# Q's first half copied in four banks by two engines, group 0's sums and first normalize moved ahead of V's projections, and group 1's values moved behind the first FFN matmuls, in the opening of a Linformer attention + squared-ReLU FFN kernel

## The chip, the cores and the metric

One core of one Trainium2 chip. The metric is device microseconds for one execution of the whole kernel. All runs told here are of the fast kind (no run was more than 1.5% above the fastest of its kernel), and the times of kernels are compared over the runs of the same rounds on the same chip.

## The reference, cut to what matters

```python
k_proj = einsum('ks,bhsd->bhkd', E, k)          # E, F: 64 x 1024; q, k, v: 8 x 8 x 1024 x 64
v_proj = einsum('ks,bhsd->bhkd', F, v)
attn   = softmax(q @ k_proj^T / sqrt(64))       # 1024 x 64 for each batch and head
x      = (attn @ v_proj) as 8192 rows of 512
out    = square(relu(x @ w_in)) @ w_out         # 512 -> 2048 -> 512
```

The attention is small. The two matrix products behind it are the work. Of the eight batches, only the first must do its attention before the FFN can begin; the others do it in the shadow of the FFN of the batch before. The first batch is cut into two halves of its columns, and only the first half of its attention stands ahead of the first FFN matmul. The change is all in that opening.

## The kernel before

The opening, in program order (in the timelines of the two kernels TensorE, VectorE and ScalarE each show their instructions in this order; where TensorE waits, what follows waits too: in the changed kernel V's projection, whose load had landed at 16.86 us (17.10 less the lag of 0.24 us, both below), starts at 18.21 us, behind sums that started at 17.98):

```python
for s in (slice(0, 4), slice(4, 8)):
    load_heads(K_first, k, s)                     # one load queue, in this order
...
load_q_half(0, slice(0, H))
for s in (slice(0, 4), slice(4, 6), slice(6, 8)):
    load_heads(V_first, v, s)
... # then w_in in pieces, the second half of Q, w_out

def half_transpose_q(self, c, g, psum):           # four heads into one PSUM bank, one copy
    ps = psum("ps_q", (P, 4, 2, P), BF16)
    for h in range(4):
        for n in range(2):
            nc.tensor.transpose(ps[:, h, n], self.Q[:, 4 * g + h, ...], ident[:])
    nc.vector.tensor_copy(qt[:, 4 * g:4 * g + 4, 2 * c:2 * c + 2], ps[:])

def first_stages(self):
    filler(2); self.project_k(0)                  # filler(n): n matmuls whose result nobody reads
    filler(1); self.transpose_k(0)
    self.project_k(1)
    filler(2); self.transpose_k(1)
    filler(1)
    for g in range(2):
        self.half_transpose_q(0, g, ffn_psum)
    for g in range(2):                            # g: four heads
        self.half_scores(0, g)
        self.half_exponentials(g)                 # ScalarE
    heads = [slice(0, 4), slice(4, 6), slice(6, 8)]
    self.project_v(heads[0])                      # waits for V's load
    self.copy_v(heads[0])
    self.half_sums(0, apart=True)                 # waits for exponential 0
    self.half_sums(1)
    self.half_reciprocals(0)                      # ScalarE: Ln, then Exp(-x)
    self.half_reciprocals(1)
    self.half_values(0)
    for s in heads[1:]:
        self.project_v(s)
        self.copy_v(s)
    self.half_values(1)
    for g in range(2):
        for e in range(2):
            self.half_normalize(0, g, e)          # VectorE; writes block 2g+e of xT
# then the FFN: the first 16 matmuls into ps_h are four output blocks, taken
# column block by column block of xT: four matmuls need only normalize (0,0),
# the next four (0,1), then (1,0), then (1,1).
```

The instructions that carry the story are: the Q transposes (`ps_q`), the scores and exponential 0, the projection of V (`ps_v`), the sums (`ps_r`), the values, and the first `ps_h`.

The softmax here doesn't subtract the row's maximum and nothing guards it: scores larger than these inputs give would overflow.

## Time and profile before

| | before |
|---|---|
| median of 3 runs | 484.47 us (483.62 to 485.47) |
| span of the profiled run | 482.4 us |
| TensorE busy | 470.3 us (97%) |
| TensorE's waits, summed | 8.3 us, all up to 21.05 us |
| first `ps_h` / 17th `ps_h` | 21.05 us / 24.70 us |

From the page of the kernel before, its first and fourth part:

```profile
## 1 busy us (share of the span) xinstructions
PE 470.3 (97%) x3630; PEld 292.6 (61%) x3630; DVE 314.1 (65%) x382; ACT 261.5 (54%) x413; POOL 34.7 (7%) x48
...
## 4 chain that ended last, share of the span: by engine, by line
PE 92%; DVE 3%; DMA 3%; ACT 1%; POOL 1%; issue 0%; POOLq 0%
```

TensorE (PE) is the limit, so a gain must be TensorE time that comes earlier. The waits of TensorE in the kernel before (columns: what waited and for what, us in total, times, longest):

```profile
PE ps_E L144 <- DVE e_bf L140: 5.0, 1, 5.0
PE ps_E L144 <- ACT e_bf L140: 1.8, 1, 1.8
PE ps_kT L271 <- DVE kp L265: 0.6, 2, 0.3
PE ps_att L307 <- DVE qT L299: 0.5, 2, 0.3
PE ps_h L459 <- DVE xT L351: 0.2, 1, 0.2
PE ps_att L320 <- DVE vp L288: 0.2, 1, 0.2
```

These six are all that the view lists, and the last of them ends at 21.05 us. TensorE's timeline of the opening (columns: start, duration, line, what it wrote and read, shapes, count; in brackets idle time before it and what ended it):

```profile
9.11 1.92 PE L262 MATMUL ps_k<-K_sb,ET 128*64 128x256 bf16 x8
...
12.00 1.06 PE L262 MATMUL ps_k<-K_sb,ET 128*64 128x256 bf16 x8
...
14.29 1.07 PE L296 MATMUL ps_q<-ident,Q_sb 128*128 128x128 bf16 x16
15.69 0.41 PE L307 MATMUL ps_att<-qT,kT 64*64 64x256 bf16 x8 [0.33 <-DVE qT L299]
...
16.82 1.06 PE L284 MATMUL ps_v<-V_sb,FT 128*64 128x256 bf16 x16
17.82 0.30 PE L320 MATMUL ps_r<-expT,ones 64*32 64x256 bf16 x8
...
18.75 1.32 PE L284 MATMUL ps_v<-V_sb,FT 128*64 128x128 bf16 x32
...
21.05 6.40 PE L459 MATMUL ps_h<-xT,w_in 128*128 128x512 bf16 x28 [0.19 <-DVE xT L351]
...
53.03 0.40 PE L180 MATMUL ps_kv<-K_sb,ET 128*64 128x512 bf16 x1
53.32 0.38 PE L181 MATMUL ps_kv<-V_sb,FT 128*64 128x512 bf16 x1
```

The first `ps_v` line starts at 16.82 us because V's load lands then. (The last two lines, `ps_kv`, belong to the projection of K and V of batch 1.) When loads land can be read from the engine that issues them (POOL), which waits for an older load to end before it issues another (1.83 us for V's first part before it issues at 17.06). Its timeline of the same run:

```profile
14.53 0.70 POOL L124 DMA_DIRECT2D w_in<-in_moe_w_in_dram  x1 [1.92 <-DMA Q_sb<-in_q_dram]
17.06 0.77 POOL L97 DMA_DIRECT2D Q_sb<-in_q_dram  x1 [1.83 <-DMA V_sb<-in_v_dram]
...
19.67 0.71 POOL L124 DMA_DIRECT2D w_in<-in_moe_w_in_dram  x1 [0.56 <-DMA V_sb<-in_v_dram]
...
22.33 0.71 POOL L124 DMA_DIRECT2D w_in<-in_moe_w_in_dram  x1 [0.52 <-DMA w_in<-in_moe_w_in_dram]
```

The engine notices V at 17.06, TensorE at 16.82: a lag of 0.24 us. So Q landed at about 14.29, V's first part at 16.82, V's last part at 19.43 (V comes in three loads), and w_in's third load (the one that the ninth `ps_h` needs) at 22.09.

### The profile page before, as it was taken

To read this page: it belongs to the slowest core of one execution; us is meant where nothing else is said; L and a number is where in the kernel's file an instruction comes from. 1 tells how busy PE (TensorE), PEld (TensorE's weight loads), DVE (VectorE), ACT (ScalarE), POOL (GpSimd) and SP (SyncE) were. 2 spreads that over 40 slices of the span, in tenths; PEclk is the share of its full clock that TensorE was granted. 3 is DMA by queue.
4 is the path that set the end of the run, shared out by engine and by line. 5 is a ranking of instruction groups with operands and counts; after the bars stand their busy time and mean duration, and the time that the engine had idled before them with its cause. 6 is when DMAs were issued, how large, how long until landed. Compare 5 with 4: busy or idle time off the path is not lost.

```text
span 482.4 us, 8423 instructions
## 1 busy us (share of the span) xinstructions
PE 470.3 (97%) x3630; PEld 292.6 (61%) x3630; DVE 314.1 (65%) x382; ACT 261.5 (54%) x413; POOL 34.7 (7%) x48
## 2 busy tenths in 40 slices
PE   4899999999999999999999999999999999999997
PEld 2544676475574746657475665747557474666656
DVE  1478955554958559493776848667494855948383
ACT  2387544758427564466635667176662756545351
POOL 6540020020020001000010000100000000000000
PEclk9999999999999999999999999999999999999999
DMA  9999989579989086941859147690702102020202
GB/s 155 203 204 207 168 181 200 137 120 229 180 128 229 12 175 88 180 94 50 153 86 227 22 115 131 91 200 1 165 11 75 25 1 88 1 88 0 88 1 87
DMA packets 72789, 55.46 MB, mean 115 GB/s; under 512 B 33968, under 2 KB 64944, under 8 KB 72752
## 3 DMA queue, kind: packets, MB, share of 16 engines
q0 software_dynamic: 30624, 29.36, 39.4%
q1 hardware_dynamic: 42128, 25.56, 21.1%
q8 instruction: 28, 0.46, 0.4%
q14 instruction: 9, 0.07, 0.0%
HBM read 59.24 MB, written 16.78 MB: 158 GB/s over the span
## 4 chain that ended last, share of the span: by engine, by line
PE 92%; DVE 3%; DMA 3%; ACT 1%; POOL 1%; issue 0%; POOLq 0%
PE ps_h L459 44%; PE ps_y L479 23%; PE ps_z L479 11%; PE ps_x L479 6%; DMA V_sb<-in_v_dram 3%; PE ps_kv L180 2%; PE ps_att L221 2%; PE ps_att L206 2%; DVE hsq L521 1%; DVE s L473 1%; PE ps_v L284 0%; DVE xT L246 0%; DVE xT L351 0%; PE ps_kv L181 0%; ACT h_relu L513 0%; POOL K_sb L93 0%
## 5 line engine op out<-in xcount | busy, mean ns | idle before, releaser
L459 PE MATMUL ps_h<-xT,w_in 128*128 128x512 bf16 x1024 | 224.8, 379 | 0.2 <-DVE xT L351 0.2
L521 DVE TENSOR_TENSOR hsq<-h_relu 128x1024 bf16<-128x1024 f32 x123 | 149.9, 1222 | 75.0 <-ACT h_relu L513 74.2
L513 ACT ACTIVATE h_relu<-ps_h 128x512 f32<-128x512 f32 x255 | 149.4, 597 | 63.4 <-PE ps_h L459 63.0
L459 PEld LDWEIGHTS <-w_in 128*128 128x128 bf16 x1024 | 99.7, 98 | 117.7 <-issue 1.9
L479 PEld LDWEIGHTS <-s 128*128 128x128 bf16 x1024 | 98.5, 98 | 19.8 <-issue 8.7
L479 PEld LDWEIGHTS <-hsq 128*128 128x128 bf16 x768 | 73.8, 98 | 17.3 <-issue 3.8
L479 PE MATMUL ps_y<-T,s 128*128 128x256 bf16 x512 | 62.4, 273 | 0.0
L246 DVE TENSOR_TENSOR xT<-ps_att,rs 128x1024 bf16<-128x1024 f32 x28 | 33.4, 1215 | 17.6 <-ACT rs L236 17.0
L473 DVE TENSOR_TENSOR s<-hsq 128x1024 bf16<-128x1024 bf16 x64 | 43.5, 683 | 0.0
L591 ACT COPY o_sb<-ps_y 128x512 f32<-128x512 f32 x15 | 8.8, 586 | 53.8 <-PE ps_y L479 53.7
L213 ACT ACTIVATE expT<-ps_att 128x1024 bf16<-128x1024 f32 x28 | 27.2, 1025 | 14.0 <-PE ps_att L206 14.0
L479 PE MATMUL ps_x<-w_out,hsq 128*128 128x256 bf16 x256 | 33.2, 273 | 0.0
L479 PE MATMUL ps_y<-w_out,hsq 128*128 128x256 bf16 x256 | 33.2, 273 | 0.0
L595 DVE TENSOR_TENSOR o_sb<-ps_z,p_b 128x512 f32<-128x512 f32 x16 | 11.0, 688 | 33.8 <-issue 19.9
L479 PE MATMUL ps_y<-T,hsq 128*128 128x256 bf16 x256 | 30.9, 272 | 0.0
L479 PE MATMUL ps_z<-T,s 128*128 128x256 bf16 x256 | 30.6, 273 | 0.0
L479 PE MATMUL ps_z<-w_out,s 128*128 128x256 bf16 x256 | 30.6, 273 | 0.0
L591 ACT COPY p_b<-ps_y 128x512 f32<-128x512 f32 (+1 forms) x17 | 9.4, 556 | 25.9 <-PE ps_y L479 25.8
L81 POOL DMA_DIRECT2D Q_sb<-in_q_dram x7 | 6.1, 876 | 227.7 <-DMA qT<-Q_sb 227.2
L473 DVE TENSOR_TENSOR s<-s,hsq 128x1024 bf16<-128x1024 bf16 x32 | 21.8, 684 | 0.3
L473 DVE TENSOR_TENSOR s<-hsq,s 128x1024 bf16<-128x1024 bf16 x32 | 21.7, 682 | 0.0
L591 ACT COPY p_a<-ps_y 128x512 f32<-128x512 f32 (+1 forms) x17 | 9.4, 561 | 21.8 <-PE ps_y L479 21.6
(75 smaller groups left out, 233.0 us busy)
## 6 DMA issues: line engine op xcount, KB each, us to landing
out_dram<-o_sb SPq DMA_DIRECT2D x30, 512.0 KB, 3.8
K_sb<-in_k_dram POOLq DMA_DIRECT2D x7, 1024.0 KB, 15.3
V_sb<-in_v_dram POOLq DMA_DIRECT2D x7, 1024.0 KB, 22.4
Q_sb<-in_q_dram POOLq DMA_DIRECT2D x7, 1024.0 KB, 9.4
w_out<-in_moe_w_out_dram POOLq DMA_DIRECT2D x4, 512.0 KB, 13.2
w_in<-in_moe_w_in_dram POOLq DMA_DIRECT2D x7, 256.0 KB, 10.0
K_sb<-in_k_dram POOLq DMA_DIRECT2D x2, 512.0 KB, 8.5
out_dram<-o_sb SPq DMA_DIRECT2D x3, 256.0 KB, 2.1
```

The lines of the kernel that those rows point to most:

```text
L180: nc.tensor.matmul(ps[0:KP, :], lhsT=ET[:, i, :], rhs=kv[:, :, i, :], start=f, stop=l)
L206: nc.tensor.matmul(ps[o, bank, :], lhsT=self.kT[r, 2 * pr + j, :], start=True, stop=True, rhs=self.qT[r, NT * (2 * pr + j):NT * (2 * pr + ...
L213: nc.scalar.activation(e[:], self.ps["s", pr][:], AF.Exp, scale=SCALE)
L221: nc.tensor.matmul(ps[32 * j:32 * j + 32, a, :], lhsT=weights(o, 4 * g + j), rhs=self.exp[2 * g + j // 2][o, bank, :], start=True, stop=Tr ...
L246: nc.vector.tensor_tensor(out=self.xT[:, 2 * g + e].rearrange("p a n t -> p a (n t)"), in0=self.ps["v", g, e][:], in1=self.rs[g][:], op=AL ...
L459: nc.tensor.matmul(ps[:], lhsT=w_in_blk(cb, fb), rhs=xT[:, cb, :, 2 * ch:2 * ch + 2], start=(cb == 0), stop=(cb == NCB - 1),)
L473: nc.vector.tensor_tensor(out=s[o][:, js], in0=x, in1=y, op=op)
L479: nc.tensor.matmul(ps[tb] if len(ps) == 2 else ps[0][:, tb], lhsT=lhs[:, j, tb * P:(tb + 1) * P], rhs=rhs[:, j], start=first and n == 0 an ...
L513: nc.scalar.activation(r[:, n], ps[:], AF.Relu)
L521: multiply = lambda: nc.vector.tensor_tensor(out=o, in0=r[:], in1=r[:], op=ALU.mult)
L591: nc.scalar.copy(to[:, t], ps)
L595: nc.vector.tensor_tensor(out=to[:, t], in0=ps, in1=more[:, t], op=ALU.add)
```

## The change

The intent: split the copies of Q over two engines and four banks, so that scores start sooner; let group 0's sums, which need only Q and K, run before V's projection; and let the first `ps_h` start behind normalize (0,0) and (0,1), with group 1's values and normalizes between the first `ps_h` matmuls. One filler ahead of the Q transposes is dropped as well.

```diff
-        def half_transpose_q(self, c, g, psum):
-            ps = psum("ps_q", (P, 4, 2, P), BF16)
-            for h in range(4):
+        def half_transpose_q(self, c, hs, psum, copy):
+            ps = psum("ps_q", (P, len(hs), 2, P), BF16)
+            for m, h in enumerate(hs):
                 for n in range(2):
                     nc.tensor.transpose(
-                        ps[:, h, n], self.Q[:, 4 * g + h, (2 * c + n) * P:(2 * c + n + 1) * P], ident[:])
+                        ps[:, m, n], self.Q[:, h, (2 * c + n) * P:(2 * c + n + 1) * P], ident[:])
             qt = self.qT[:].rearrange("p (h n) t -> p h n t", n=NT)
-            nc.vector.tensor_copy(qt[:, 4 * g:4 * g + 4, 2 * c:2 * c + 2], ps[:])
+            copy(qt[:, hs.start:hs.stop, 2 * c:2 * c + 2], ps[:])
@@ first_stages
             self.transpose_k(1)
-            filler(1)
-            for g in range(2):
-                self.half_transpose_q(0, g, ffn_psum)
+            for n in range(4):
+                self.half_transpose_q(
+                    0, range(2 * n, 2 * n + 2), ffn_psum, nc.scalar.copy if n == 1 else nc.vector.tensor_copy)
             for g in range(2):
                 self.half_scores(0, g)
                 self.half_exponentials(g)
             heads = [slice(0, 4), slice(4, 6), slice(6, 8)]
+            self.half_sums(0, apart=True)
             self.project_v(heads[0])
             self.copy_v(heads[0])
-            self.half_sums(0, apart=True)
             self.half_sums(1)
             self.half_reciprocals(0)
             self.half_reciprocals(1)
             self.half_values(0)
+            self.half_normalize(0, 0, 0)
             for s in heads[1:]:
                 self.project_v(s)
                 self.copy_v(s)
+            self.half_normalize(0, 0, 1)
+
+        def last_of_first(self):
             self.half_values(1)
-            for g in range(2):
-                for e in range(2):
-                    self.half_normalize(0, g, e)
+            for e in range(2):
+                self.half_normalize(0, 1, e)
@@ SECOND_HALF (what is called ahead of which step of the FFN)
-        7: "second_half 0 0", ...
+        1: "last_of_first", 7: "second_half 0 0", ...
```

(The second half's call of `half_transpose_q` is adapted and does what it did.)

## The prediction

> **What bounds the kernel.** TensorE: 470.3 us busy of a span of 482.4 (page), and 92% of the chain of waits that ended last. The view of TensorE's waits lists 8.4 us of idle time in the whole run, all before the first `ps_h` matmul at 21.05 us; from 21.05 to 37.40 TensorE is busy 16.22 of 16.35 us, from 60 to 440 us 379.89 of 380 (windows). So the change, which touches only the first 40 us, can gain no more than it brings forward the moment from which TensorE runs feed-forward matmuls without a gap.
>
> **What leads up to that moment (timeline).** Q transposes 14.29 (Q's load lands about then), two VectorE copies of 128x1024 14.95 to 16.24, scores 15.69 and 16.29, exponentials on ScalarE 16.15 to 18.09, V's projection 16.82 (waits for V's load), values of group 0 18.41, V's last heads 19.43 to 20.09, their copy until 20.40, values of group 1 until 20.87, first normalize 20.32, first `ps_h` 21.05.
>
> **What the change does, costed.**
> - Q copies: one filler less (no gain: Q lands when it ended). Four 128x512 copies, VectorE about 0.42 each, ScalarE 0.59 (the ET and FT copies of this shape). Heads 0-1 are ready about 15.2, heads 2-3 only at 15.6, ScalarE being the slower copier; the first exponential starts about 16.0 instead of 16.15.
> - Group 0's sums ahead of V: they wait for exponential 0 (about 17.05), and TensorE takes matmuls in order, so V's projection moves from 16.82 to about 17.25: 0.4 us lost for V, its copies and values. [...]
> - Normalize (0,0) moves ahead of the last V copies: about 19.35, 1 us earlier.
> - The first four `ps_h` matmuls (4 x 0.217) start right behind V's projection, which now ends about 20.5 instead of 20.05. Values of group 1 (about 0.4 us of issue) run behind them, their normalizes hidden under `ps_h`.
>
> Result: first `ps_h` about 20.5, one 0.4 us interruption, so the fifth output block (17th `ps_h`) starts about 24.35 instead of 24.70. Net gain about 0.3 us, 0.07%, all on the critical path. With half the loss to V it would be 0.5; if normalizes (1,0), (1,1) (0.65 us each) come late, 0.1.
>
> **Limit from below.** w_in's loads are nearly just in time: from when the issuing engine's waits for slots end, less the 0.24 us lag seen for V, I estimate landings at 20.1, 20.75, 22.1, 23.35, 24.6. A start earlier by over 0.5 us would wait for them.
>
> **Predicted: 484.1 us, 8 in 10 between 483.2 and 485.0**; the spread of before's runs (483.62 to 485.47) is larger than the effect. Faster by over 2%: 0.005; within 2%: 0.99; slower: 0.005.
>
> **What would show it.** Timeline: V's projection starts at 17.1 to 17.4, released by ScalarE (not by V's load); first exponential 15.9 to 16.1; first `ps_h` 20.3 to 20.8; values of group 1 between the fourth and fifth `ps_h`; the 17th `ps_h` at 24.2 to 24.5. From 40 us on both traces are the same but for the shift.
>
> **What would make it wrong.** V's or w_in's loads landing later than estimated (TensorE then waits for a DMA after 20 us); new PSUM waits (the fourth `ps_h` needs the bank of V's last copy); ScalarE's copy being quicker than 0.59; a later stage of the first batch absorbing the shift.

The sum came to a first `ps_h` at about 20.5 us and a 17th at about 24.35 instead of 24.70, a net gain of about 0.3 us. The order is seen in the timeline of the changed kernel below (sums at 17.98 us after a wait of 0.73 us, V's projection behind them at 18.21).

## The result, and the profile after

| | before | after |
|---|---|---|
| median | 484.18 us (6 runs, 483.19 to 485.47) | 484.28 us (6 runs, 484.0 to 485.07) |
| ratio | | 1.0004, 95% interval 0.9986 to 1.0022 |
| span of the profiled run | 482.4 us | 482.8 us |
| first Q transpose | 14.29 us | 15.19 us |
| first `ps_h` / 17th `ps_h` | 21.05 / 24.70 us | 21.16 / 25.34 us |

A ratio here is the mean time of one kernel's runs over the mean of the other's of the same rounds, so it is not quite the ratio of the medians. The interval of 0.0036 is 1.7 us wide, six times the predicted gain, so the time alone neither confirms nor denies a gain of 0.3 us.

From the page of the changed kernel, its first part:

```profile
## 1 busy us (share of the span) xinstructions
PE 471.1 (98%) x3629; PEld 292.7 (61%) x3629; DVE 314.4 (65%) x383; ACT 261.9 (54%) x414; POOL 34.4 (7%) x48
```

The waits of TensorE in the changed kernel:

```profile
PE ps_E L144 <- DVE e_bf L140: 5.6, 1, 5.6
PE ps_E L144 <- ACT e_bf L140: 0.8, 1, 0.8
PE ps_r L320 <- ACT expT L314: 0.7, 1, 0.7
PE ps_k L262 <- DMA K_sb<-in_k_dram: 0.4, 1, 0.4
PE ps_att L320 <- DVE vp L288: 0.3, 1, 0.3
PE ps_kT L271 <- DVE kp L265: 0.2, 1, 0.2
```

The waits for the copies of Q (0.5) and for the first normalize (0.2) are gone as intended, and a new one has come: the sums wait 0.7 us for exponential 0. TensorE's timeline of the changed kernel:

```profile
9.10 1.87 PE L262 MATMUL ps_k<-K_sb,ET 128*64 128x256 bf16 x8 [0.38 <-DMA K_sb<-in_k_dram]
...
12.05 1.91 PE L262 MATMUL ps_k<-K_sb,ET 128*64 128x256 bf16 x8
...
15.19 1.14 PE L296 MATMUL ps_q<-ident,Q_sb 128*128 128x128 bf16 x16
16.26 1.00 PE L307 MATMUL ps_att<-qT,kT 64*64 64x256 bf16 x16
17.98 0.30 PE L320 MATMUL ps_r<-expT,ones 64*32 64x256 bf16 x8 [0.73 <-ACT expT L314]
18.21 1.06 PE L284 MATMUL ps_v<-V_sb,FT 128*64 128x256 bf16 x16
...
20.14 1.08 PE L284 MATMUL ps_v<-V_sb,FT 128*64 128x128 bf16 x32
21.16 1.04 PE L464 MATMUL ps_h<-xT,w_in 128*128 128x512 bf16 x4
22.12 0.41 PE L320 MATMUL ps_att<-expT,vp 64*32 64x256 bf16 x16
22.47 5.63 PE L464 MATMUL ps_h<-xT,w_in 128*128 128x512 bf16 x24
...
53.67 0.40 PE L180 MATMUL ps_kv<-K_sb,ET 128*64 128x512 bf16 x1
53.67 0.40 PE L181 MATMUL ps_kv<-V_sb,FT 128*64 128x512 bf16 x1
```

And the issuing engine:

```profile
14.58 0.70 POOL L124 DMA_DIRECT2D w_in<-in_moe_w_in_dram  x1 [1.99 <-DMA Q_sb<-in_q_dram]
17.10 0.77 POOL L97 DMA_DIRECT2D Q_sb<-in_q_dram  x1 [1.82 <-DMA V_sb<-in_v_dram]
...
22.29 0.71 POOL L124 DMA_DIRECT2D w_in<-in_moe_w_in_dram  x1 [0.49 <-DMA w_in<-in_moe_w_in_dram]
```

The loads of Q, V and w_in landed within 0.05 us of the run before. But the second projection of K, which the change does not touch and which stands ahead of everything it does touch, took 1.91 us in place of 1.06. The Q transposes therefore began 0.90 us later, 0.85 us after Q had landed (the slower fillers and transposes behind that projection cost another 0.25 us, and the filler that the change drops gave 0.24 back). Counted from that start, the 17th `ps_h` comes after 10.15 us (25.34 - 15.19) where it took 10.41 us (24.70 - 14.29): 0.26 us less. Behind it, the way to the end of the trace is 0.24 us shorter, which lies in the K and V projection of batch 1 (2.10 us before, 1.85 after, in the chain of waits). The sum: + 0.90 - 0.26 - 0.24 = + 0.40 us, the difference of the spans.

Why is that projection shorter? In the kernel before, its first matmul on V starts 0.29 us after the one on K, at 53.32 us; V's load for batch 1 was issued at 30.31 us and landed 22.96 us later, at 53.27. In the changed kernel the load landed at 52.82 us, before TensorE came, and the two matmuls start together. The kernel before was thus waiting for a load here, although the view of the waits does not list it (the matmul on K still counts as busy). An opening that was 0.3 us faster would have met the same load, and gained nothing behind it unless the load came sooner too. All 14 profiles of this document show the same picture: in six of them (`before`, `after_again`, `before_qlate`, `vfirst_qlate`, `vfirst`, `vfirst_pelate_nolast`) the matmul on V starts 0.04 to 0.05 us after this landing and 0.06 to 0.29 us after the one on K; in the other eight the load is there already and they start within 0.01 us of each other. From the first `ps_x` matmul behind this projection to the end, 13 of the 14 traces take 427.22 to 427.26 us.

Why 1.91 and 1.06? Between the starts of two such matmuls lie (1.91 - 0.42) / 7 = 0.21 us in the slow and (1.06 - 0.27) / 7 = 0.11 us in the fast case (0.42 and 0.27 us are what the last of the eight takes by itself). Both paces are found in one run as well: in after_warm (below) the first K projection took 1.06 us, in windows in which the clock reads 1.00, and the second 1.92 us, at a clock of 0.55 in the window of 12 to 15 us. So I read the slow pace as that of a slow clock. The clock row of the page does not show the slow phase of the two kernels compared here (it reads 9 tenths there, and windows of 8 to 26 us read 1.00 in both kernels), so it has to be read from the durations. The packed trace shows why: its clock records begin only with the first rise, at 11.23 us in the kernel before and at 15.38 us in the changed one, and what lies ahead of them counts as full clock. These two moments agree with the reading: the second K projection starts at 12.00 us, after the rise, in the one, and at 12.05 us, before it, in the other. Over all 14 profiles the first rise lies between 5.49 and 15.38 us; what sets it no run here shows.

### The profile page after: what moved, and what is told of

Its sections match the earlier page's. It is cut to its first block, busy times and chain, and to the rows that moved or that the text cites. A ratio compares the mean times of both kernels' runs of the same rounds, so it can differ in the third digit from the quotient of the medians.

```text
span 482.8 us, 8424 instructions
## 1 busy us (share of the span) xinstructions
PE 471.1 (98%) x3629; PEld 292.7 (61%) x3629; DVE 314.4 (65%) x383; ACT 261.9 (54%) x414; POOL 34.4 (7%) x48
## 4 chain that ended last, share of the span: by engine, by line
PE 94%; DVE 3%; DMA 2%; ACT 1%; issue 0%; POOLq 0%
PE ps_h L464 44%; PE ps_y L484 23%; PE ps_z L484 11%; PE ps_x L484 6%; PE ps_kv L180 3%; PE ps_att L221 2%; DMA K_sb<-in_k_dram 2%; PE ps_att L206 2%; DVE hsq L526 1%; PE ps_k L262 1%; DVE s L478 1%; DVE xT L246 0%; PE ps_v L284 0%; ACT h_relu L518 0%; DVE xT L351 0%
## 6 DMA issues: line engine op xcount, KB each, us to landing
w_in<-in_moe_w_in_dram POOLq DMA_DIRECT2D x7, 256.0 KB, 10.1
```

## The experiments

Two measures from each trace, with all times counted from the first Q transpose of the same trace:
- **D**, until the ninth `ps_h` is due: the start of the stretch with the fifth to eighth `ps_h`, plus 4 x 0.217 us (where the eight follow without a break, the start of the first plus 1.74). It holds all that the change moves, and no wait for w_in's third load. (It does hold a small wait for w_in's second load where TensorE is on time in the changed kernels: the third `ps_h` comes up to 0.12 us late in after_qlate, vfirst and vfirst_qlate.)
- until the 17th `ps_h` starts, which does hold that wait.

"Late" is how long after Q's landing the transposes began; V's first part lands 2.48 to 2.53 us after Q in all 14 profiles. The table comes first; the runs follow.

| kernel | late | D | to the 17th `ps_h` | w_in's third load after Q | ratio to before (95%) |
|---|---|---|---|---|---|
| before | 0.00 | 8.50 | 10.41 | 7.80 | |
| after | 0.85 | 8.15 | 10.15 | 7.71 | 1.0004 (0.9986 to 1.0022) |
| after_again | 0.26 | 8.08 | 10.64 | 8.96 | 0.9995 (0.9982 to 1.0007) |
| before_warm | 2.03 | 8.10 | 10.02 | 7.69 | 0.9989 (0.9977 to 1.0001) |
| after_warm | 0.44 | 8.17 | 10.18 | 7.70 | 0.9994 (0.9981 to 1.0007) |
| warm_vfirst | 1.24 | 7.74 | 9.75 | 8.33 | 0.9985 (0.9972 to 0.9998) |
| before_qlate | 0.00 | 8.57 | 10.82 | 8.87 | 1.0035 (1.0021 to 1.0048) |
| after_qlate | 0.00 | 8.21 | 10.49 | 8.54 | 1.0027 (1.0012 to 1.0042) |
| vfirst_qlate | 0.00 | 8.21 | 10.77 | 8.82 | 1.0033 (1.0019 to 1.0047) |
| vfirst | 0.15 | 8.02 | 10.47 | 8.68 | 1.0006 (0.9994 to 1.0019) |
| before_pelate | 1.16 | 8.10 | 10.01 | 7.69 | 1.0004 (0.9986 to 1.0022) |
| after_pelate | 1.53 | 8.07 | 10.07 | 7.79 | 1.0024 (1.0004 to 1.0044) |
| vfirst_pelate_nolast | 0.95 | 8.04 | 9.96 | 8.61 | 1.0011 (0.9986 to 1.0036) |
| vfirst_pelate_dveq | 1.04 | 7.73 | 9.74 | 7.77 | 1.0010 (0.9989 to 1.0030) |

All outputs are right. Each row is one profiled execution; D repeats within 0.1 us for the same kernel and the same side of the "late" column (vfirst, 0.15 us late, lies between its two sides), while the times of one kernel's runs in the same rounds spread by up to 2.4 us.

### after_again: the changed kernel once more

No edit.

> The changed kernel, unchanged, once more. Theory A (clock phase): the change brings the gap-free start about 0.3 us forward, but the profiled run of it drew a late warm-up of TensorE's clock (second K projection 1.91 us against 1.06 us before), which cost about 0.9 us; the phase is drawn anew in each run. Then this profile shows one of two pictures: second K projection about 1.06 us with the first ps_h at 20.3 to 20.8 and the 17th ps_h at 24.2 to 24.5; or 1.9 us with about 21.2 and 25.3. Rival B (the change itself costs, by making V's projection wait for exponential 0, and the clock has nothing to do with it): the 17th ps_h at 25.2 to 25.5 whatever the K projection takes. Time: ratio 0.999 to 1.001 under both, as the spread of single runs is about 1 us.

Median 484.33 us against 484.71. The profile showed neither of my two pictures: the second K projection took 1.54 us, between the two; the first `ps_h` came at 21.06, and the 17th at 25.80, later than either. The rise of the clock is thus not one of two moments: by its 1.54 us it fell within this projection (an estimate from the two paces), and over the 14 profiles it lies between 5.49 and 15.38 us. What held up the `ps_h` is worth reading closely. The chain of waits of this run names VectorE's normalize:

```profile
22.58 1.30 DVE xT L351 x2
23.88 1.88 PE ps_h L464 x8
```

But that piece holds two normalizes, the first of which (0.69 us long in the trace) was done by 23.3, and the ninth `ps_h` needs only the first. In the same run the issuing engine has:

```profile
24.10 0.71 POOL L124 DMA_DIRECT2D w_in<-in_moe_w_in_dram  x1 [1.72 <-DMA w_in<-in_moe_w_in_dram]
```

Less the lag of 0.24 us this is 23.86, the moment at which the timeline has TensorE start. The wait was for w_in's third load, 8.96 us after Q, over a microsecond later than in the two first profiles. My rival B predicted a 17th `ps_h` at 25.2 to 25.5 whatever K's projection took; measured from the transposes, D is 8.08, so it is not the change that delays.

### before_warm and after_warm: matmuls on a constant tile from 1.5 us on

```diff
+    wtile = const_pool.tile([P, 512], BF16, name="wtile"); nc.vector.memset(wtile[:], 1.0)
+    def warm(n):  # n matmuls of wtile with itself, into a PSUM bank that nobody reads
     def E_and_F():
+        warm(8)
         ... transposes of E
+        warm(5)
         ... transposes of F
-            filler(2)
+            filler(4)
             self.project_k(0)
```

> The kernel before with matmuls on a constant tile ahead of and between the transposes of E and F, so that TensorE is busy from about 1.5 us. Theory A: both K projections about 1.06 us in every run; since V's load sets the pace, the first ps_h stays at 20.9 to 21.1 and the 17th at 24.6 to 24.8; time 483.5 to 484.2 with a spread of runs below 1 us. Rival B: nothing changes, the spread stays about 2 us.

> The changed kernel with the same early matmuls. Theory A: K projections about 1.06 us, V's projection at 17.1 to 17.4 released by exponential 0, first ps_h 20.3 to 20.7, 17th ps_h 24.2 to 24.5, that is 0.3 us ahead of before_warm, and 0.3 us in time (0.06%), which the interval may not resolve. Rival B: 17th ps_h no earlier than in before_warm.

As a way to fix the clock this failed, and so did my expectation of where `ps_h` would stand (21.59 and 21.48 us; the 17th at 25.25 and 25.67). The runs still spread by 1.1 us (before_warm, median 484.42) and 1.7 us (after_warm, 484.40). In before_warm TensorE was kept busy from 1.50 us, yet the five matmuls from 6.21 us still took 2.32 us (0.43 each), and the first K projection had to wait for the slow fillers (four in 1.89 us; in after_warm in 1.04); the transposes began 2.03 us after Q. In after_warm the same five took 1.25 us from 6.19 us on, at the fast pace, and the clock fell back later. Up to there both had run the same instructions at the same times within 0.02 us, with one gap of 0.48 us, and yet the clock records begin with a first rise at 5.49 us in after_warm and at 10.91 us in before_warm. Windows of after_warm (columns: the stretch, then busy time of each engine, then PEclk, DMA share, GB/s):

```profile
6.00:9.00 3.00, 3.00 (x22) 1.43 (x20) 0.42 (x1) 1.45 (x2) 1.78 (x3) 1.00 1.13 174
9.00:12.00 3.00, 1.69 (x14) 1.06 (x13) 0.68 (x3) 0.00 (x0) 0.70 (x1) 1.00 1.35 200
12.00:15.00 3.00, 2.65 (x10) 1.37 (x10) 0.89 (x3) 0.00 (x0) 0.71 (x1) 0.55 1.32 205
```

Here the clock is at 0.55 (at half from 12.31 to 15.72 us in the packed trace's clock records), after a stretch in which TensorE was busy 1.69 of 3 us, with waits for K (0.79 us), for VectorE (0.44) and again for K (0.43, into the next stretch); the second K projection took 1.92 us. That these waits made the clock fall is not shown; no run here tests it. By accident the pair was useful: in before_warm V had landed long before it was wanted, and D was 8.10 in place of 8.50. So the 8.50 of the kernel before holds 0.4 us of waiting for V that only a punctual TensorE has to do. It is V's last part that sets this: in the kernel before, the last 16 matmuls of V's projection start 5.14 us after the transposes, when that part lands (19.43 us), and in before_warm 4.76 us after them, with no wait. With both kernels late (8.10 and 8.17), the change brought nothing up to the ninth `ps_h`.

### warm_vfirst: group 0's sums back behind V's first projection

```diff
-            self.half_sums(0, apart=True)
             self.project_v(heads[0])
             self.copy_v(heads[0])
+            self.half_sums(0, apart=True)
```
(on after_warm)

> after_warm with group 0's sums put back behind V's first projection and its copy: takes out the one move that I hold to cost something. Theory A: V's projection back at 16.8 to 16.9 (released by V's load), first ps_h 20.05 to 20.3; the third ps_h may wait for w_in's second load (estimated landing 20.75), so the 17th ps_h at 24.0 to 24.2, 0.1 to 0.3 us ahead of after_warm. If sums ahead of V were what gains, it would be later than in after_warm.

D fell from 8.17 to 7.74: the sums' place costs 0.43 us here, more than the 0.1 to 0.3 us that I expected of the 17th `ps_h` (that one, too, came 0.43 us sooner after the transposes, 9.75 against 10.18). By the clock the first `ps_h` started at 20.38, a little outside 20.05 to 20.3, and V's projection at 16.73 us was not held by V's load, as V had landed 0.6 us before; its place right behind the scores was what it gained. The time, 484.11 us against 484.71, has a ratio whose interval just stays below 1 (0.9985, 0.9972 to 0.9998). It is the only such result, and the same order without the early matmuls (vfirst, below) did not repeat it.

### before_qlate, after_qlate, vfirst_qlate: TensorE ready before Q lands

```diff
+    spare = hsq_pool.tile([P, 2, HFB, TCH], BF16, name="hsq")
+    nc.gpsimd.dma_start(spare[:, 0, 0:2], rows(k, 0)[:, 0:2])     # nobody reads it
     load_q_half(0, slice(0, H))
```
(on before, after, and after with the sums moved back as in warm_vfirst)

> A spare load of two heads of K (a quarter of K) ahead of Q's load, so that Q and V land about 1.25 us later and TensorE stands ready when Q lands, whatever its clock did. Theory A' (formed after the first four runs: V lands a constant 2.5 us after Q; the kernel before runs max(V's landing + 7.9, start of the Q transposes + 10.0) until the 17th ps_h, the changed one start of the Q transposes + 10.15; so the change gains 0.26 us only while TensorE takes Q up at once, and loses about 0.1 when it comes late to Q, by a cold clock or a late K): transposes to 17th ps_h 10.3 to 10.5 us, V's projection released by V's load. Rival B (the change is worth a constant amount, run-to-run noise hides it): 10.0 to 10.1, as in before_warm. Time about 1 us longer than before.

> The changed kernel with the same spare load. Theory A': transposes to 17th ps_h 10.1 to 10.3 us, 0.2 to 0.3 less than in before_qlate, V's projection 0.4 us behind V's landing and released by exponential 0. Rival B': (the change is worth nothing anywhere) same as before_qlate within 0.05.

> The changed kernel with group 0's sums back behind V's first projection, and the spare load. Theory A': V's last heads land 5.1 us after Q, so the first ps_h comes 5.7 to 5.9 us after the start of the transposes, may wait for w_in's second load, and the 17th comes 10.0 to 10.2 us after; so here the sums' place costs almost nothing (0 to 0.15 us against after_qlate). If the sums ahead of V cost 0.4 us everywhere: 9.75.

The setting did what it should: TensorE waited for Q in all three. V's projection in before_qlate began at V's landing (18.04 us, 2.53 after the transposes) and in after_qlate behind the sums. The 17th `ps_h` missed the expected figures in all three (10.82, 10.49, 10.77), because w_in's third load landed 8.5 to 8.9 us after Q and not 7.8. The ninth `ps_h` of after_qlate, in TensorE's timeline:

```profile
22.52 1.04 PE L466 MATMUL ps_h<-xT,w_in 128*128 128x512 bf16 x4
23.73 2.53 PE L466 MATMUL ps_h<-xT,w_in 128*128 128x512 bf16 x10 [0.17 <-DMA w_in<-in_moe_w_in_dram]
```

The transposes stand at 15.51 us in before_qlate and at 15.18 in after_qlate, and the first of before_qlate's eight unbroken `ps_h` at 22.34. D is free of the third load: 8.57, 8.21, 8.21. When TensorE is punctual the change gains 0.36 us up to there, and where the sums stand makes no difference, as expected: V's last part, then w_in's second load, are waited for in vfirst_qlate, and the third `ps_h` comes 6.46 us after the transposes in both. But then the third load decides. The 17th `ps_h` comes 0.33 us sooner in after_qlate than in before_qlate, which is just by how much sooner the third load landed (8.54 and 8.87), so no profile shows the 0.36 us kept to the 17th. The spare load itself cost all three 1.3 to 1.7 us of time (ratios 1.0027 to 1.0035), about the time that it holds the queue (1.25 us in the issuing engine's waits).

### vfirst: sums moved back, nothing else

> The changed kernel with group 0's sums back behind V's first projection, nothing else. Theory A': transposes to 17th ps_h 9.7 to 10.2 us depending on how late TensorE comes to Q, never later than in the changed kernel for the same lateness; time 0.2 to 0.5 us below before (ratio 0.9990 to 0.9996), at the edge of what the interval can resolve. If the sums' place costs nothing: as the changed kernel, 10.15.

TensorE took up Q 0.15 us after it landed. D was 8.02, better than the kernel before by 0.48; then the ninth `ps_h` waited 0.34 us for w_in's third load, and the 17th came at 10.47, outside the expected 9.7 to 10.2 and no better than the kernel before in its profile (10.41). The time, 484.03 against 483.66, ratio 1.0006 (0.9994 to 1.0019), excludes a gain of more than 0.06%, about 0.3 us: the expected 0.9990 to 0.9996 holds only at its edge.

### before_pelate, after_pelate, vfirst_pelate_nolast, vfirst_pelate_dveq: TensorE always late to Q

```diff
             self.transpose_k(1)
+            filler(4)
```
(on before and after; vfirst_pelate_nolast in addition moves the sums back and calls `last_of_first` at the end of `first_stages`, so that the first `ps_h` again waits for all; vfirst_pelate_dveq moves the sums back and copies all four parts of Q with `nc.vector.tensor_copy`)

> Four more filler matmuls ahead of the Q transposes make TensorE come 0.9 us or more late to Q in every run, so that V has landed (2.5 us after Q) before it is wanted and w_in's loads are in time. Measure: from the first Q transpose to the moment at which the ninth ps_h is due (start of the run of ps_h that holds the fifth to eighth, plus 0.87 us for four; call it D). Theory A' (before is bound by V's landing when TensorE is on time, by the Q chain when late): D = 8.05 to 8.15 us (8.10 in before_warm), no wait of V's projection for a load. If V's load binds here too: 8.5.

> The changed kernel with the same fillers. Theory A': D = 8.10 to 8.20 us, so no gain, a loss of 0 to 0.1 us against before_pelate: the wait of TensorE for exponential 0 (0.7 us) eats what the early ps_h bring. Rival (the change gains 0.3 us in every regime, as predicted): 7.75 to 7.85.

> The changed kernel with group 0's sums back behind V's first projection and with group 1's values and normalizes back ahead of the first ps_h, same fillers. The early ps_h alone is undone against warm_vfirst (D = 7.74). If the early start of ps_h is what gains: D = 8.0 to 8.15. If the early normalize of group 0 alone gains, it stays at 7.7 to 7.8.

> The changed kernel with group 0's sums back behind V's first projection and all four Q copies on VectorE, same fillers. Three copies in a row took 1.20 us on VectorE, so the second would end 1.3 us after the first transpose, as ScalarE's does. Expected: exponential 0 starts 1.65 to 1.75 us after the first transpose as with ScalarE, D = 7.7 to 7.8 as in warm_vfirst. If sharing the copies with ScalarE is what speeds up the scores: 0.2 to 0.4 later.

D: 8.10 (8.05 to 8.15 expected), 8.07 (8.10 to 8.20, so just below), 8.04 (8.0 to 8.15), 7.73 (7.7 to 7.8). The rival, a gain of 0.3 us in every case, would have had 7.75 to 7.85 for after_pelate. The new wait of TensorE in after_pelate, which has no counterpart in before_pelate, is the same line as in the changed kernel (the lines around it give D):

```profile
15.30 1.06 PE L296 MATMUL ps_q<-ident,Q_sb 128*128 128x128 bf16 x16
...
18.01 0.30 PE L320 MATMUL ps_r<-expT,ones 64*32 64x256 bf16 x8 [0.73 <-ACT expT L314]
...
22.50 3.69 PE L465 MATMUL ps_h<-xT,w_in 128*128 128x512 bf16 x15
```

In before_pelate the two lines that give D are:

```profile
14.82 1.06 PE L296 MATMUL ps_q<-ident,Q_sb 128*128 128x128 bf16 x16
...
21.18 5.11 PE L460 MATMUL ps_h<-xT,w_in 128*128 128x512 bf16 x22 [0.19 <-DVE xT L351]
```

Against vfirst_pelate_dveq and warm_vfirst, vfirst_pelate_nolast undoes the early `ps_h`, and loses 0.3 us: it is the early `ps_h` that gain. (Each of the two differs from it in one thing more, the engine of one copy and the place of the extra matmuls; both give the same D, 7.73 and 7.74.) What is left of the change then (four copies, the early normalize) is worth 8.10 - 8.04 = 0.06 us. That is a net figure: TensorE waits 0.60 us in vfirst_pelate_nolast for V's last copies, which now stand behind the early normalize on VectorE. In vfirst_pelate_dveq exponential 0 started 1.58 us after the first transpose (1.65 to 1.75 expected), in after_pelate 1.63: giving a copy to ScalarE brings nothing for the scores. ScalarE's copy took 0.58 to 0.59 us for 512 elements, four on VectorE 1.42 us together.

One result stays open: the times of after_pelate (484.82 to 486.29, median 485.35) lie 1 us above those of before_pelate (484.36), though both profiled spans are 482.8 us. In the profile of before_pelate 0.56 us were lost far behind the opening, at 132 us, where the projection of batch 3 waited for V's load (`PE ps_kv L181 <- DMA V_sb<-in_v_dram` in its waits); no other profile has that. Of the unprofiled runs only the time is known; their warm-up and landings are not.

## Why the prediction was right or wrong

- **The time**: right, 484.28 us against a predicted 484.1 with a range of 483.2 to 485.0, and a ratio of 1.0004. The text said that the spread of runs is larger than the effect, and it is. This says nothing for the mechanism: the range would have held a gain of 0.3 us, none, or a loss of 0.3 us alike.
- **TensorE as the limit, and the opening as the only place to gain**: right. From the 17th `ps_h` on, the two traces differ by 0.24 us in all, and that is a wait for a load of batch 1 (below).
- **The length of the changed chain**: right up to V's projection, when counted from the Q transposes, and right in sum. V's projection predicted 2.96 us after them (17.25 - 14.29), measured 3.02; exponential 0 1.71 and 1.71; first `ps_h` 6.2 and 5.97; 17th `ps_h` 10.06 and 10.15. The last agreement is partly luck: the first `ps_h` came 0.24 us sooner than costed, and from it to the 17th passed 4.18 us where 3.85 were costed (16 `ps_h` at 0.217 us make 3.47, but in the kernel before they took 3.65 with nothing between them). The loss of V to the sums and the gain of the early `ps_h` were both real, 0.34 to 0.43 us (D of 8.07 and 8.17 against 7.73 and 7.74) and 0.3 us.
- **The times on the clock in "What would show it"**: wrong, all of them late by 0.7 to 1.0 us against the figures costed (17.25, 16.0, 20.5, 24.35), and by 0.4 to 0.8 us beyond the ranges. V's projection at 17.1 to 17.4 was 18.21; the first exponential at 15.9 to 16.1 was 16.90; the first `ps_h` at 20.3 to 20.8 was 21.16; the 17th at 24.2 to 24.5 was 25.34. The step that failed is the first one: "Q transposes 14.29 (Q's load lands about then)", taken as the fixed origin. That Q and TensorE were ready at the same moment was a coincidence of the one profile. In the changed kernel's profile TensorE's clock was slow through the second K projection, 1.91 us in place of 1.06, and the transposes began 0.90 us later.
- **"Net gain about 0.3 us ... all on the critical path"**: not so, for two reasons. The first lies in the opening, where three limits stand side by side: V's last part (it holds the kernel before to D = 8.5 when TensorE is punctual), the chain from the Q transposes (D = 8.10 before, 8.07 to 8.21 after), and w_in's third load. A punctual TensorE gains 0.36 us up to the ninth `ps_h`; a late one gains nothing (8.10 and 8.07), because the kernel before then no longer waits for V, while the changed kernel still stops 0.7 us for exponential 0. The profile of before already held the warning: eight matmuls that took 1.92 us once and 1.06 us the next time, upstream of everything that I took as fixed. The second reason lies behind the opening: V's load for batch 1, which in the kernel before already held its projection by 0.29 us. It landed 38.4 to 39.5 us after Q in the 14 profiles, so that a 17th `ps_h` earlier than 10.1 to 11.2 us after Q (an estimate: less the 28.3 us that lie between the 17th `ps_h` and that projection) gains nothing to the end. The prediction named "a later stage of the first batch absorbing the shift" among what could make it wrong; it is the first stage of batch 1 that does.
- **"A start earlier by over 0.5 us would wait for them"**: the w_in loads do limit from below, but closer. I estimated the third to land 7.8 us after Q; seven of 14 profiles have it at 7.7 to 7.8, the other seven at 8.3 to 9.0. In the late ones it takes away part or all of the gain. What delays it in those was not found; V's first part (2.5 us after Q) does not vary. Nor is it this load alone: in three of the other seven (before_warm, before_pelate, after_pelate) the issuing engine sees the fourth load 2.0 to 2.4 us after the third, where it is 1.3 in the kernel before.

So where did 0.3 us go? In the two profiles compared, into the later start of the Q transposes; and had they started on time, V's load for batch 1, as it landed in the kernel before, would have taken what was left. To be seen in the time, the gain needs TensorE on time for Q, w_in's third load on time, and batch 1's V on time; no profile of the changed kernel shows all three together, so this is argued from the limits and not shown. How often each is the case in unprofiled runs no trace here tells; the mean over the runs is 0 within about 0.2%. No version tried beats both kernels beyond doubt: the one with the sums moved back is ahead in D whenever TensorE is late, but its time was not shown to be lower (ratios 0.9985 with the early matmuls and 1.0006 without).

## What to carry to other kernels

A time read from one profile of a kernel's first 20 us is a draw: before costing a change there, ask what each start was waiting for, and by how much the second-last limit was behind; a gain on the last one alone is worth only that margin. Then look for the next load behind it that lands just in time: here it stood 28 us later, and the view of the waits did not list it. Measure such a change from an event inside the trace (here the Q transposes) and not from the start of the span. And when an instruction is moved ahead on an engine whose instructions stay in program order, as TensorE's do in the timelines here, check that its inputs are ready there: sums that waited 0.7 us for an exponential held up a projection whose data had already landed, and moving them back behind it gave back about 0.4 us whenever TensorE was late.
